# Attention and soft mixture of experts on one core: split diagonal blocks in the last batch, and a background piece that may wait for a change of matmul row form

## The chip, the cores and the metric

The kernel runs on one core of a Trainium2 chip. All times are device microseconds (us) of one execution; the clock of TensorE in the tables is the share of full speed that was granted. PE is TensorE, DVE is VectorE, ACT is ScalarE, SP is SyncE, whose queue issues every DMA of this kernel.

## The reference

```
u, v: (8, 2496, 256)   z: (8, 2496, 64)   phi: (256, 32)
w1: (8, 256, 1024)     w2: (8, 1024, 256)

attn = relu(z @ z.T / 2496) ** 2            # per batch, symmetric
x    = (u * (attn @ v)).reshape(19968, 256)

logits = x @ phi
d = softmax of logits over the tokens (columns), c = softmax over the 32 slots (rows)
slots = d.T @ x                             # 32 slots of 256, 4 for each of 8 experts
slots = per expert: relu(slots @ w1[e]) @ w2[e]
out   = c @ slots                           # (19968, 256) float32
```

## The kernel before, in words

**Chunks, blocks and half steps.** Each of the 8 batches has five chunks of queries (512, the last 448 wide) and five blocks of 512 keys. A block is worked off in two *half steps* of 256 keys, so a chunk has 10 half steps, a batch 50, the program 410 (the last batch's last chunk is cut in two). A half step consists of `prepare(k)`, which makes the squared scores of half k, and of the sums of `acc` over its keys. `prepare` runs three half steps ahead of the sums (two at the very start). Products are split in a high and a low part (`ph`, `pl`, and v and z alike), so each is three matmuls.

**Symmetry.** Scores of a block and chunk off the diagonal are made once; DVE transposes them (`y`), `store` writes them to DRAM (`turned_<chunk>_<block>`), and when the mirrored chunk needs them they are fetched (`r<-turned`). Such a half is `turned` and has no score matmuls. In the table `MEETS` a chunk's row gives the order of its key blocks. A block in the diagonal that is written as two pairs, as `(1, 0)` and `(1, 1)`, is in split form: its first half *lends* (DVE transposes the half that its mirror can use, `yd`, and `lend` stores it, `lent<-yd`), its second half *borrows* (`rd<-lent`) and makes scores over 256 queries instead of 512. `MEETS[0]` (batches 1 to 6, and most of batch 0) has all diagonals in split form, `MEETS[1]` (the last batch, whose blocks go in the order 4, 0, 1, 2, 3) none.

**Row forms of PE.** Where the half prepared in a step has scores of its own, the step's sums are `sums_halves`: pairs of matmuls over 64 rows, with the scores (64 rows too) between. Where it is turned, they are `sums_whole`: matmuls over 128 rows. In the timeline the tile column tells the form, 64\*128 or 128\*128.

**Background work.** As soon as 1024 tokens of x are complete, `groups(q)` puts 15 pieces in the list `work`: logits, the exponentials, four transposes of x and one of the weights, four shifts between other pieces, and a closing piece. One piece is taken in each half step but the first two of a chunk. A `shift` is four DMAs of 72 KB, `xt<-y`, on SP. The closing piece puts `slot_sums` in `late`; these products with `xt` are run by PE inside the *next* group's logits, after its own 32 matmuls, and need all four shifts of their group:

```
            if late:
                late.pop()(ps)
...
            todo = [logits, ex, *blocks, e, shifts[0], c0, shifts[1], c1, shifts[2], c2, shifts[3]]
            todo.append(lambda: (c3(), late.append(slot_sums)))
```

Logits and slot sums have a third form, 64\*32. From the last shift to the next group's logits are the closing piece and whatever time the list is empty. `logits` is always the first of its group.

**Order.** Every engine's instructions run in program order (`InOrder`), so a waiting instruction holds up all that follow on its engine. On SP stand, in a half step's order, what `transfers(h)` issues: u, fetches of turned and borrowed halves up to eight steps ahead, loads of the next batch's z and v (`splits`), stores; then the step's shift. `FIRST_Z` says after which half step the first batch's z blocks are split into high and low parts (two casts on ACT and two subtractions on DVE each).

Before the change all engine instructions stand under the helper's line L64, after it under L67.

Of the kernel before, what the change touches and what calls it, by code (L numbers as in the profile page):

```python
# [33 lines left out]
CATCH = 18  # L34
# [3 lines left out]
MEETS = (  # L38
# [3 lines left out]
)  # L42
FIRST_MEETS = ((0, 1, 2, 3, 4), (1, 0, 2, 4, 3)) + MEETS[0][2:]

FIRST_Z = {8: 1, 9: 2, 10: 4, 11: 3}

RAW_SCORES = 12

PAD = 224

# [17 lines left out]
def attn_soft_moe_kernel(ctx, tc, uT, v, zz, phi, ww, outT):  # L68
# [93 lines left out]
    def constants():  # L162
        make_identity(nc, ident)


        nc.gpsimd.memset(rsel, 0.0)
        for h in range(4):
            rows = slice(h * NS, (h + 1) * NS)
            nc.gpsimd.tensor_copy(ssel[rows], ident[rows, rows])
        for h in range(2):  # L170
            for r in range(4):
                nc.gpsimd.tensor_copy(
                    rsel[:, h, r, 16 * h : 16 * h + 16].rearrange("k (j s) -> k j s", s=SE),
                    ident.rearrange("k (j q) -> k j q", q=NS)[:, :, 0:SE],
                )
        sp.dma_start(phi_sb, phi.rearrange("(c p) s -> p c s", p=P))
        nc.gpsimd.memset(one, 1.0)
# [38 lines left out]
    halves = []  # L216
# [21 lines left out]
    def run(todo):  # L238
        now, todo[:] = todo[:], []
        for f in now:  # L240
            f()
# [17 lines left out]
    def scores(k):  # L259
# [21 lines left out]

        if k < RAW_SCORES:
            for h, rows in enumerate(HALF):
# [133 lines left out]
    def sums_halves(k, acc, phase, before):  # L417


        x = halves[k]  # L420
        todo = [[], []]
        hi, lo = pend[k]
        for t, kt in enumerate(x.tiles):
            vt = vt_[x.b, kt // 2][:, kt % 2]
            hh, lh, hl = (vt[:, 0], hi[:, t]), (vt[:, 1], hi[:, t]), (vt[:, 0], lo[:, t])
            if kt < KT - 1:
                for h in range(2):
                    todo[h] += [hh, lh, hl]
            else:

                todo[0] += [hh] if phase else [hh, lh]
                todo[1] += [hl] if phase else [lh, hl]
        for i in range(len(todo[0])):
            for h, rows in enumerate(HALF):
                vp, pp = todo[h][i]
                c = h ^ phase ^ side[0]
                mm = pe.matmul(
                    totals(acc, c, x), vp[rows, c * P : (c + 1) * P], columns(pp[rows], x),
                    start=(x.begins and phase == 0 and i == 0),
                    stop=(x.ends and phase == 1 and i == len(todo[0]) - 1),  # L440
                )
                if before is not None:
                    await_(mm, before)
                    before = None
        if phase == 0:
            turn = nc.gpsimd.nop()
            await_(turn, mm)
            return turn
        side[0] ^= 1

    def sums_whole(k, acc):

        x = halves[k]
        hi, lo = pend[k]
        for t, kt in enumerate(x.tiles):
            assert kt < KT - 1
            vt = vt_[x.b, kt // 2][:, kt % 2]
            for c in range(2):
                for i, (l, r) in enumerate(((0, hi), (1, hi), (0, lo))):
                    pe.matmul(  # L460
                        totals(acc, c, x), vt[:, l, c * P : (c + 1) * P], columns(r[:, t], x),
                        start=(x.begins and t == 0 and i == 0),
                        stop=(x.ends and t == 1 and i == 2),
                    )
# [41 lines left out]
    def groups(q):  # L506
# [103 lines left out]
        def turn_x_whole(i):  # L610
            j, t0 = i // 2, i % 2 * 2
            ps = ms_ps.tile([P, 2, 512], F32, tag="ms", name=f"xt_{q}_{i}")
            for k in range(2):
                turn_x(ps[:, k], x, 4 * j + t0 + k)
            for k in range(2):
                copy_x(act.copy, ps[:, k, 0:D], xt[:, t0 + k, j * D : (j + 1) * D])
# [38 lines left out]
        rest = lambda: None  # L655
        if q < NQG - 2:

            todo = [logits, ex, *blocks, e, shifts[0], c0, shifts[1], c1, shifts[2], c2, shifts[3]]
            todo.append(lambda: (c3(), late.append(slot_sums)))
        else:  # L660


            todo = [rest, rest, logits, ex, lambda: behind.append(adding.pop(0)), lambda: behind.append(add_counts)]
            todo += [c0, c1, c2, c3, turn_e_whole, *[lambda i=i: turn_x_whole(i) for i in range(4)]]
            todo.append(lambda: late.append(last_slot_sums))
# [69 lines left out]
    def weights(left):  # L735

        if left in W_TAKES:
            W_TAKES[left]()
        for i in W_LOADS.get(left, ()):
            load_w(i)  # L740
# [11 lines left out]
    work = []  # L752
# [14 lines left out]
    def transfers(h):  # L767

        x = halves[h]
        if x.at == 2:  # L770
            load_u(x.b, x.ch)
        for k in range(h + 1, min(h + 9, len(halves))):
            y = halves[k]

            if y.turned and y.opens and k not in arriving and k not in fetched:
                if k - h <= 7 and (y.b, y.p, y.ch[0]) in scratch:
                    fetched.add(k)
                    fetch(k)
            if y.borrows and k - h <= 5 and k not in fetched and (y.b, y.p, y.p) in scratch:
                fetched.add(k)  # L780
                borrow(k)
        for f, b, i in splits.get(h + 2, ()):
            if (b, 0) not in vt_:
                take_blocks(b)
            landing.setdefault(h + 2, []).append(f(b, i))
        while stores and stores[0][0] <= h + 1:
            stores.pop(0)[1]()

    def split_first_v():
        if v_splits:  # L790
            v_splits.pop(0)()
            open_loads(NRAW)
# [3 lines left out]
    def between_last(k):  # L796

        if k:
            if k == 1:
                xps.append(sc_ps.tile([P, 2, QC], F32, tag="sc", name="tr_first"))  # L800
                two = [raws.tile([P, 2, D], F32, tag="raw", name=f"xt_last_{i}", bufs=NRAW) for i in range(2)]
                xt_last.extend(t[:, i] for t in two for i in range(2))
            ps = xps[0][:, k - 1, 0:D]
            turn_x(ps, xg_[NQG - 1], k - 1)
            copy_x(act.copy, ps, xt_last[k - 1])
# [7 lines left out]
    def keep_busy(n):  # L813
        for _ in range(n):
            for h, rows in enumerate(HALF):
                pe.matmul(idle[:, h], zero[rows, 0:P], zero[rows], start=True, stop=True)
# [7 lines left out]
    prepare(1)  # L824
    keep_busy(5)
    constants()
    acc = None
    for h, x in enumerate(halves):
        if x.begins:
            acc = acc_ps.tile([P, 2, QC], F32, tag="acc", name=f"acc_{x.ch[3]}")  # L830
        last = len(halves) - h
        transfers(h)
        weights(last)
        for f in landing.pop(h, ()):
            behind.append(f)
        if work and (x.at > 1 or last <= 20):
            work.pop(0)()
        ahead = [k for k in range(h + 2 + (h > CATCH), h + 3 + (h >= CATCH)) if k < len(halves)]
        split_first_v()
        if ahead and not halves[ahead[0]].turned:  # L840
            turn = sums_halves(h, acc, 0, None)
            prepare(ahead.pop(0))
            sums_halves(h, acc, 1, turn)
        else:
            if ahead and not x.ends:
                prepare(ahead.pop(0))
            elif not ahead:
                run(middle)
                run(behind)
                between_last(3 - last)  # L850
            sums_whole(h, acc)
        if x.ends:
            finish_chunk(x.b, x.ch, acc)
        for k in ahead:
            prepare(k)
        if h in FIRST_Z:
            z_splits.pop(FIRST_Z[h])()
        del pend[h]
# [281 lines left out]
```

## Time and profile before

| | before |
|---|---|
| median of 3 runs | 1359.67 us (1359.03 to 1361.28) |
| the profiled execution | 1361.58 us |
| its span | 1359.8 us |
| mean granted clock of TensorE | 0.984 |
| busy: PE, DVE, ACT | 1336.1, 1084.2, 908.7 us |
| PE, sums of `acc` with the high and the low part | 988.4 and 622.7 us |
| PE, scores `sc` of two blocks and of one | 131.5 and 54.7 us |
| DMA: mean rate, written and read in HBM | 219 GB/s, 112.98 and 161.25 MB |
| `xt<-y`: DMAs, KB each, median from issue to landing | 288, 72.0, 3.4 us |
| `turned<-y`: the same | 320, 256.0, 4.4 us |
| `lent<-yd`: the same | 132, 64.0, 2.5 us |

In a row of the timeline stand the start, the duration, the engine, the line, the operation, what it writes and reads, the tile form, and how many instructions were drawn together; in brackets stands how long the engine was idle ahead of it and what ended that. Durations of matmuls overlap, so the pitch is read from the starts. A row of windows gives for each engine the busy time and the count, and at its end the granted clock, the busy share of the DMA engines and GB/s. PE is busy in 9 tenths or more of every one of 40 slices but the last two.

### The profile page before, as it was taken

What the parts mean: (1) busy time and instruction counts of PE and PEld (TensorE: products, weight loads), DVE (VectorE), ACT (ScalarE), POOL (GpSimd) and SP (SyncE); (2) the same over time, 40 slices, a digit from 0 to 9 for tenths busy, and PEclk for the clock granted to TensorE, in tenths of its full rate; (3) what the DMA queues carried; (4) which work ended last, traced back from release to release, by engine and by line L of the source; (5) the groups of instructions that cost most, each with busy time, mean ns of one, the idle gap of its engine ahead of it and who ended that gap; (6) DMA issues with size and microseconds to landing.
All of it is one profiled execution on the core that took longest, in us unless ns stands there. A gap on an engine that the chain in (4) does not pass through costs nothing.

```text
span 1359.8 us, 27351 instructions
## 1 busy us (share of the span) xinstructions
PE 1336.1 (98%) x10929; PEld 1062.3 (78%) x10929; DVE 1084.2 (80%) x1444; ACT 908.7 (67%) x1093; POOL 3.7 (0%) x22
## 2 busy tenths in 40 slices
PE   9999999999999999999999999999999999999985
PEld 6777887778777888778877788778877788778952
DVE  7878897779868898688987889797986889876563
ACT  8866686668755687566856678566875668654453
POOL 0000000000000000000000000000000000000000
PEclk9999999999999999999999999999999999999985
DMA  6568677675758667686776666777585776769969
GB/s 204 158 186 253 206 191 223 196 242 162 221 172 286 211 161 211 183 255 204 191 225 190 230 202 165 226 240 256 142 237 164 243 234 176 219 167 303 361 271 378
DMA packets 132511, 297.28 MB, mean 219 GB/s; under 512 B 17440, under 2 KB 36896, under 8 KB 120608
## 3 DMA queue, kind: packets, MB, share of 16 engines
q1 hardware_dynamic: 132384, 295.54, 70.6%
q8 instruction: 86, 1.41, 0.4%
q14 instruction: 41, 0.34, 0.1%
HBM read 161.25 MB, written 112.98 MB: 202 GB/s over the span
## 4 chain that ended last, share of the span: by engine, by line
PE 92%; ACT 2%; DMA 2%; DVE 2%; SPq 1%; issue 1%; DVEq 0%; ACTq 0%
PE acc L64 74%; PE sc L64 11%; PE lg L64 2%; PE pf L64 2%; SPq L64 1%; ACT r L64 1%; ACT ot L64 1%; PE po L64 1%; DMA lent<-yd 1%; PE h L64 1%; DMA outT<-ot 1%; DMA vr<-in_v 0%; ACT ph L64 0%; DVE pl L64 0%; PE idle L64 0%
## 5 line engine op out<-in xcount | busy, mean ns | idle before, releaser
L64 PE MATMUL acc<-ph,v 64*128 64x512 f32 (+5 forms) x5036 | 988.4, 387 | 0.0
L64 PEld LDWEIGHTS acc<-ph,v 64*128 64x128 f32 (+1 forms) x5036 | 593.5, 185 | 146.5 <-issue 24.9
L64 PE MATMUL acc<-pl,v 64*128 64x512 f32 (+5 forms) x2518 | 622.7, 383 | 1.5 <-DVE pl L64 1.5
L64 DVE TENSOR_TENSOR pl<-r,ph 128x1024 fp32r<-128x1024 f32 (+1 forms) x412 | 468.5, 1145 | 118.2 <-ACT ph L64 107.7
L64 ACT ACTIVATE r<-sc 128x1024 f32<-128x1024 f32 (+1 forms) x244 | 232.7, 954 | 194.6 <-PE sc L64 185.9
L64 ACT CAST ph<-r 128x1024 fp32r<-128x1024 f32 (+1 forms) x285 | 290.2, 1023 | 108.5 <-PE acc L64 77.1
L64 PEld LDWEIGHTS acc<-pl,v 64*128 64x128 f32 (+1 forms) x2518 | 306.8, 185 | 62.9 <-DVE pl L64 4.4
L64 ACT ACTIVATE r<-r 128x1024 f32<-128x1024 f32 (+1 forms) x244 | 241.1, 988 | 7.0
L64 DVE STREAM_TRANSPOSE y<-r 128x1024 f32<-128x1024 f32 x160 | 198.1, 1238 | 0.0
L64 PE MATMUL sc<-z,z 64*128 64x512 f32 x912 | 131.5, 393 | 0.2 <-ACT r L64 0.2
L64 DVE CAST ph<-r 128x1024 fp32r<-128x1024 f32 (+1 forms) x127 | 76.0, 598 | 40.9 <-ACT r L64 38.7
L64 PEld LDWEIGHTS sc<-z,z 64*128 64x128 f32 x912 | 85.0, 184 | 20.8 <-ACT r L64 0.6
L64 ACT CAST z<-zr 64x512 fp32r<-64x512 f32 x70 | 43.3, 619 | 56.2 <-DMA zr<-in_zz 55.0
L64 DVE TENSOR_TENSOR xg<-acc,ut 128x1024 f32<-128x1024 f32 (+7 forms) x57 | 48.4, 872 | 34.3 <-PE acc L64 34.3
L64 DVE TENSOR_TENSOR z<-zr,z 64x512 fp32r<-64x512 f32 x70 | 48.1, 687 | 21.5 <-ACT z L64 19.7
L64 DVE TENSOR_TENSOR v<-vr,v 128x512 fp32r<-128x512 f32 x80 | 53.6, 669 | 11.2 <-ACT v L64 11.1
L64 ACT CAST v<-vr 128x512 fp32r<-128x512 f32 x79 | 48.4, 613 | 17.9 <-DMA vr<-in_v 17.9
L64 PE MATMUL sc<-z 64*128 64x512 f32 (+1 forms) x468 | 54.7, 339 | 0.0
L64 DVE STREAM_TRANSPOSE y<-xg 128x512 f32<-128x512 f32 x72 | 49.5, 688 | 0.0
L64 PEld LDWEIGHTS sc<-z 64*128 64x128 f32 x468 | 41.1, 184 | 7.7
L64 DVE COPY ot<-pf 128x1024 f32<-128x1024 f32 (+2 forms) x22 | 24.3, 1103 | 21.9 <-PE pf L64 20.8
L64 ACT COPY ot<-pf 128x1024 f32<-128x1024 f32 (+2 forms) x22 | 20.1, 915 | 26.2 <-PE pf L64 24.7
(149 smaller groups left out, 481.0 us busy)
## 6 DMA issues: line engine op xcount, KB each, us to landing
turned<-y SPq DMA_DIRECT2D x320, 256.0 KB, 4.4
r<-turned SPq DMA_DIRECT2D x76, 1024.0 KB, 6.3
xt<-y SPq DMA_DIRECT2D x288, 72.0 KB, 3.4
vr<-in_v SPq DMA_DIRECT2D x80, 256.0 KB, 3.8
outT<-ot SPq DMA_DIRECT2D x16, 1024.0 KB, 6.9
ut<-in_uT SPq DMA_DIRECT2D x31, 512.0 KB, 5.3
zr<-in_zz SPq DMA_DIRECT2D x35, 256.0 KB, 5.5
lent<-yd SPq DMA_DIRECT2D x132, 64.0 KB, 2.5
```

Source lines behind the costliest of these rows:

```text
L64: return lambda *a, **k: self.tc.keep_in_program_order(f(*a, **k))
```

## The change

Three tables and one rule. In `MEETS[1]` three chunks of the last batch (their diagonal blocks 0, 1 and 2) get split diagonals, which also changes the order of their blocks. Two z splits of the first batch come one and two half steps later. And the logits of the groups 0 to 17 may now wait in the list, with all pieces behind them, for up to `HOLD` half steps, if within that time a half step comes whose row form differs from that of the step before (`switch`); they are run in that step.

```diff
-    ((0, 1, 2, 4, 3), (0, 4, 1, 2, 3), (0, 4, 1, 2, 3), (4, 2, 3, 0, 1), (0, 1, 2, 4, 3), (4, 3, 0, 1, 2)),
+    ((0, 1, 2, 4, 3), ((0, 0), 1, 4, 2, 3, (0, 1)), (0, (1, 0), 4, 2, 3, (1, 1)),
+     ((2, 0), 4, 3, (2, 1), 0, 1), (0, 1, 2, 4, 3), (4, 3, 0, 1, 2)),
...
-FIRST_Z = {8: 1, 9: 2, 10: 4, 11: 3}
+FIRST_Z = {8: 1, 9: 2, 11: 4, 13: 3}
...
+HOLD = 4
...
+            logits.meets_switch = True
             todo = [logits, ex, *blocks, e, shifts[0], c0, shifts[1], c1, shifts[2], c2, shifts[3]]
...
+    def ahead_of(h):
+        return [k for k in range(h + 2 + (h > CATCH), h + 3 + (h >= CATCH)) if k < len(halves)]
+
+    whole = [not k or halves[k[0]].turned for k in map(ahead_of, range(len(halves)))]
+    switch = [i and whole[i] != whole[i - 1] for i in range(len(halves))]
+    held = 0
...
         if work and (x.at > 1 or last <= 20):
-            work.pop(0)()
-        ahead = [k for k in range(h + 2 + (h > CATCH), h + 3 + (h >= CATCH)) if k < len(halves)]
+            if hasattr(work[0], "meets_switch") and True in switch[h : h + 1 + HOLD - held] and not switch[h]:
+                held += 1
+            else:
+                held = 0
+                work.pop(0)()
+        ahead = ahead_of(h)
```

The numbers behind the names are running numbers of tiles and differ between the programs. First PE, at the logits of group 4 in batch 2, chunk 1 (`lg_...<-xg` are its own products, `lg_...<-xt` the slot sums of group 3). Before:

```order
L64 MATMUL acc_4399<-ph_4335,v_4_3159 128x512 x4
L64 MATMUL acc_4399<-pl_4336,v_4_3159 128x512 x2
L64 MATMUL lg_4492<-xg_3567,phi_sb 32x256 x16
L64 MATMUL lg_4492<-xt 32x256 x16
L64 MATMUL acc_4399<-ph_4377,v_5_3160 128x512 x4
L64 MATMUL acc_4399<-pl_4378,v_5_3160 128x512 x2
```

After:

```order
L67 MATMUL acc_4390<-ph_4462,v_8_3163 128x512 x4
L67 MATMUL acc_4390<-pl_4463,v_8_3163 128x512 x2
L67 MATMUL lg_4622<-xg_3567,phi_sb 32x256 x16
L67 MATMUL lg_4622<-xt 32x256 x16
L67 MATMUL acc_4390<-ph_4506,v_6_3161 128x512 x2
L67 MATMUL acc_4390<-pl_4507,v_6_3161 128x512
```

The logits moved three half steps on, from between two steps of 64-row pairs (x4 and x2 on both sides) to the place where the pairs change to 128-row products (x2 and x1 behind).

Second SP, at the same place. Before, in batch 2:

```order
L64 DMA lent_1_4307<-yd_4297 32x4x128 x4
L64 DMA r_4441<-turned_0_1_3983 128x2048
L64 DMA turned_1_2_4443<-y_4339 32x4x512 x4
L64 DMA ut_4488<-in_uT 128x2x512
L64 DMA rd_4490<-lent_1_4307 128x512
L64 DMA r_4576<-turned_0_2_4076 128x2048
L64 DMA turned_1_4_4578<-y_4427 32x4x512 x4
L64 DMA r_4663<-turned_1_2_4443 128x2048
```

After, in batch 2:

```order
L67 DMA xt<-y_3878 32x576 x4
L67 DMA r_4432<-turned_0_1_3976 128x2048
L67 DMA turned_1_2_4434<-y_4327 32x4x512 x4
L67 DMA ut_4479<-in_uT 128x2x512
L67 DMA rd_4481<-lent_1_4294 128x512
L67 DMA r_4528<-turned_0_2_4067 128x2048
L67 DMA turned_1_4_4530<-y_4418 32x4x512 x4
L67 DMA xt<-y_3878 32x576 x4
L67 DMA r_4615<-turned_1_2_4434 128x2048
```

Before, in batch 3:

```order
L64 DMA xt<-y_6102 32x576 x4
L64 DMA r_6379<-turned_0_1_5890 128x2048
L64 DMA turned_1_2_6381<-y_6277 32x4x512 x4
L64 DMA ut_6426<-in_uT 128x2x512
L64 DMA rd_6428<-lent_1_6245 128x512
L64 DMA r_6474<-turned_0_2_6023 128x2048
L64 DMA turned_1_4_6476<-y_6365 32x4x512 x4
L64 DMA xt<-y_6102 32x576 x4
L64 DMA r_6561<-turned_1_2_6381 128x2048
```

The last two shifts of group 3 moved to this place in batch 2, where in the program before no shift stood; the order is now that of batch 3 before. The second shift shown is the one for which the slot sums in `lg_4622` wait.

## The prediction

> **What bounds the kernel now.** I read the busy times first: TensorE works for 98% of the span, so until the tail time is lost or won only where PE gets fewer columns, changes form less often, or stands still.
>
> ```profile
> PE 1336.1 (98%) x10929; PEld 1062.3 (78%) x10929; DVE 1084.2 (80%) x1444; ACT 908.7 (67%) x1093; POOL 3.7 (0%) x22
> L64 DVE STREAM_TRANSPOSE y<-r 128x1024 f32<-128x1024 f32 x160 | 198.1, 1238 | 0.0
> ```
>
> Then the timeline of PE. A change of row form has a price: two pairs at full pitch follow each other every 0.233 us (a 128-row product, or two 64-row ones). From 237.25 to 237.57 are 0.32 instead of 0.233, and 237.57 to 238.14 takes 0.57 for four 64-row products instead of 0.467, so this change from 128 to 64 rows costs 0.19. The logits and slot sums have a third form (64*32) and stand here inside a half step of 64-row sums.
>
> ```profile
> 237.25 0.39 PE L64 MATMUL acc<-pl,v 128*128 128x512 f32 x1
> 237.57 0.73 PE L64 MATMUL acc<-ph,v 64*128 64x512 f32 x4
> 238.14 0.39 PE L64 MATMUL acc<-pl,v 64*128 64x512 f32 x2
> ...
> 241.27 1.09 PE L64 MATMUL lg<-xg,phi_sb 64*32 64x256 f32 x32
> 242.16 1.07 PE L64 MATMUL lg<-xt 64*32 64x256 f32 x32
> ```
>
> The next rows give the way back (380.04 to 380.37 is 0.33, and 380.37 to 380.94 is 0.57: 0.20 together) and the price of score products over 512 and over 256 columns: six take 0.86 and 0.52.
>
> ```profile
> 375.46 0.86 PE L64 MATMUL sc<-z,z 64*128 64x512 f32 x6
> ...
> 378.50 0.52 PE L64 MATMUL sc<-z 64*128 64x256 f32 x6
> ...
> 380.04 0.40 PE L64 MATMUL acc<-pl,v 64*128 64x512 f32 x2
> 380.37 0.73 PE L64 MATMUL acc<-ph,v 128*128 128x512 f32 x2
> 380.94 0.39 PE L64 MATMUL acc<-pl,v 128*128 128x512 f32 x1
> ```
>
> Last, the waits. The only stall of PE near 1 us in mid-program is at 793, where a load of v went out at 783.83 because SP was busy with four shifts for 4.26 ahead of it; ACT waits 3.40 for its landing, DVE follows, and PE loses 1.07:
>
> ```profile
> 778.90 4.26 SPq L64 DMA_DIRECT2D xt<-y  x4
> ...
> 783.83 0.92 SPq L64 DMA_DIRECT2D vr<-in_v  x2
> ...
> 789.34 0.62 ACT L64 CAST v<-vr 128x512 fp32r<-128x512 f32 x1 [3.40 <-DMA vr<-in_v]
> 793.14 0.47 PE L64 MATMUL acc<-pl,v 64*128 64x448 f32 x2 [1.07 <-DVE pl L64]
> ```
>
> **The change part by part.** *Row form.* Counted in the order of the two programs, PE changes between whole and half steps, or to the logits and back inside one form, 115 times before and 106 after (11 logits come to stand at a change that is there anyway; the new order of the last batch has 2 changes more). 9 x 0.20 = -1.8 us; bounds -1.7 and -1.8 by the two prices.
>
> *Narrow diagonals.* Three second halves have six score products of 256 columns instead of 512: 3 x (0.86 - 0.52) = -1.0, all on PE's path. In return each lends and borrows: a half-wide transpose on DVE (half of 1.238), some smaller casts, four 64 KB stores and one fetch on SP. DVE's and ACT's cover is the slack of the last batch, 160.0 - 124.4 and 160.0 - 101.5:
>
> ```profile
> 1116.00:1276.00 160.00, 159.79 (x1395) 131.65 (x1392) 124.42 (x176) 101.45 (x126) 0.00 (x0) 1.00 0.76 227
> ```
>
> I cost it at nothing; without cover it would be three times about 0.6. The borrowed half comes five or more half steps after the lending one, so the stores have time.
>
> *Two z splits moved* (block 4 one half step later, block 3 two). A split is two subtractions on DVE, 1.40. Block 3's now falls between the casts of halves 15 and 16, where the remainder is ready at 63.84 + 1.23 = 65.07 and PE takes it at 66.03:
>
> ```profile
> 51.93 1.40 DVE L64 TENSOR_TENSOR z<-cw,z 64x512 fp32r<-64x512 f32 x2
> ...
> 63.84 1.23 DVE L64 TENSOR_TENSOR pl<-r,ph 128x1024 fp32r<-128x1024 f32 x1
> ```
> ```profile
> 66.03 0.40 PE L64 MATMUL acc<-pl,v 64*128 64x512 f32 x2
> ```
>
> 1.40 against 0.96 of slack: +0.4, bounds 0 (DVE has gaps just ahead) and +1.4.
>
> *The stall at 793.* The background pieces of the batches 2, 4 and 6 come later, so this shift no longer stands ahead of that load: -1.1, bounds -1.1 and 0 (another shift may meet another load).
>
> These four give -1.8 - 1.0 + 0.4 - 1.1 = -3.5.
>
> *The held logits.* A logits piece may wait up to four half steps for a change of form. Held with it are the other 14 pieces of its group and of the next one, since one list feeds one piece per half step. But inside the logits of group q PE also runs the slot sums of group q-1, which need the four DMAs of that group's last shift. Before, the last shift was issued at least five half steps ahead of them. Now the catching up runs the other way: when a group is late and the next logits then meet a change at once, only the closing piece of the old group stands between. By the order after, the distance is 9 for five groups, 4 or 5 for seven, and only **2 half steps** for the groups 4, 9, 14 (first type) and 5, 10, 15 (second type). All of PE is queued behind those slot sums, in program order: the sums of the half, its scores, and after them ACT, DVE and the next stores.
>
> The price of two half steps is in the trace: in the batches 3 and 5 of before, SP has at the same place of the batch (chunk 1) the very order that batches 2, 4 and 6 get now: shift, fetch, `turned_1_2`, fetch, `turned_1_4`, shift. PE comes to the change where the logits would stand at 538.27 in batch 3, and reaches slot sums 0.89 later (242.16 - 241.27): 539.16.
>
> ```profile
> 524.86 0.59 SPq L64 DMA_DIRECT2D xt<-y  x1
> 525.49 0.58 SPq L64 DMA_DIRECT2D r<-turned  x1
> 526.17 2.27 SPq L64 DMA_DIRECT2D turned<-y  x4
> ...
> 536.43 0.33 SPq L64 DMA_DIRECT2D r<-turned  x1
> 536.86 2.30 SPq L64 DMA_DIRECT2D turned<-y  x4
> 539.20 4.44 SPq L64 DMA_DIRECT2D xt<-y  x4
> ```
> ```profile
> 538.27 0.73 PE L64 MATMUL acc<-ph,v 128*128 128x512 f32 x2
> ```
> ```profile
> L64 SPq DMA_DIRECT2D xt<-y x4: 519/890/2004, 539.2 to 543.0; - x4
> DMA to landing us min/median/max: 3.3/5.6/6.5
> ```
>
> The last of the four shifts is issued at 543.0 and lands at 546.3 at the earliest (shortest landing 3.3): PE would stand 546.3 - 539.16 = 7.1. In batch 5 the same from 857.09 + 0.89 = 857.98 to 861.4 + 2.2 = 863.6: 5.6.
>
> ```profile
> 857.09 0.73 PE L64 MATMUL acc<-ph,v 128*128 128x512 f32 x2
> ```
> ```profile
> L64 SPq DMA_DIRECT2D xt<-y x4: 588/854/2022, 857.5 to 861.4; - x4
> DMA to landing us min/median/max: 2.2/3.0/5.3
> ```
>
> Mean 6.4, three times: **+19.1**. The lower bound is batch 2 itself in before, where `turned_1_4` was issued earlier:
>
> ```profile
> 373.94 4.03 SPq L64 DMA_DIRECT2D turned<-y  x4
> ```
>
> A shift behind it starts at 377.97, its last DMA 3.8 later (543.0 - 539.2), and lands 2.2 on, at 384.0; PE at 380.37 + 0.89 = 381.26: 2.7. I take 6.4, since there the row ahead of the store is a shift, as it will be, and here a store. For the second type the odd batches again have a shift at the place:
>
> ```profile
> 598.00 0.73 PE L64 MATMUL acc<-ph,v 64*128 64x512 f32 x4
> ```
> ```profile
> L64 SPq DMA_DIRECT2D xt<-y x4: 588/588/924, 595.2 to 597.5; - x4
> DMA to landing us min/median/max: 2.7/3.4/4.4
> ```
>
> 597.5 + 2.7 = 600.2 against 598.00 + 0.89 = 598.89: 1.3 each, **+3.9**; bounds 0 (the shift takes its turn a little sooner) and 597.5 + 4.4 - 598.89 = 3.0.
>
> The Trainium skill prices this landing too ("DMA: Bandwidth & Descriptors", the section on the fixed and variable cost): about 2.0 us plus the bytes at 436 GB/s, so by estimate 2.2 for 72 KB. By it the first stall would be 543.0 + 2.2 - 539.16 = 6.0 instead of 7.1 and the total about 1.7 lower; batch 3's own shortest landing is 3.3, so I keep the rows.
>
> *What a stall does afterwards.* The clock (third value from the end of a row of windows) shows it in the tail: a stretch in which PE worked 2.32 of 3.40 us is followed by one at 0.51, then full speed. The stall at 793, with 2.67 of 3.40 worked, left it at 1.00.
>
> ```profile
> 789.40:792.80 3.40, 2.67 (x15) 1.85 (x13) 2.75 (x5) 2.84 (x5) 0.00 (x0) 1.00 1.05 331
> ```
> ```profile
> 1303.10:1306.50 3.40, 2.32 (x41) 1.39 (x43) 1.87 (x4) 1.44 (x3) 0.00 (x0) 1.00 0.13 51
> 1306.50:1309.90 3.40, 3.40 (x30) 1.95 (x30) 1.25 (x2) 1.01 (x1) 0.00 (x0) 0.51 0.65 258
> 1309.90:1313.30 3.40, 3.40 (x62) 2.08 (x62) 2.31 (x2) 2.02 (x2) 0.00 (x0) 0.99 1.01 417
> ```
>
> So after each stall of the first type I expect 3.4 us at half clock, which lose 1.7: 3 x 1.7 = **+5.1**, bounds 0 and, if the shorter stalls of the second type do it too, 10.2. Stalls of 1.3 lie between the two rows and nearer the first, so I take none for them.
>
> **Sum.** -3.5 + 19.1 + 3.9 + 5.1 = +24.6 on the profiled execution, whose time is 1361.58 (span 1359.8). That is 1.91 above the median of the runs, so in their terms 1359.67 + 24.6 = **1384.3**.
>
> **Rivals.** *The clock does not fall.* All as above without the 5.1: 1379.2. For it: 1.07 us at 793 did nothing. Against: the row at 1306.50.
>
> *Short stalls.* The fetch ahead of `turned_1_4` is not held up, so the first type stands 2.7: 1384.3 - 3 x 3.7 = 1373.2, and 1368.1 if the clock stays. For it: batch 2 in before. Against: the batches with the order of after. The Trainium skill ("TensorE: Matmul & The Clock Gate", "HAM oscillation") would let the clock fall only for PE gaps over about 3.4 us. By that rule short stalls keep the clock and give this second time, 1368.1; the tail, where 1.08 of 3.40 was idle ahead of the half clock, speaks against it.
>
> *No stall: faster.* SP issues the last shift as soon as its data is there, so that its last DMA goes out by 539.16 - 2.2 = 537.0 in batch 3's time and no slot sums wait. Then only the -3.5 is left (1356.2), and from that point on every us later is paid three times. For it: SP waits in these places, so it has room. Against: six us are missing in both batches, with the same order.
>
> *The hold does nothing* can be excluded: the order of the changed program has the logits moved.
>
> **Chances.** Stalls with a fall of the clock as summed 0.50; without it 0.20; short stalls 0.19; no stall 0.07; a little of everything that cancels 0.04. The range reaches from short stalls whose clock falls at some of the three (1370) to all first-type stalls at 7.1 with a second half-clock stretch after the second type (about 1384.3 + 2.1 + 5.1 = 1391.5): 1370 to 1392. Anything within 0.2% (2.7 us, about what a measurement tells from no change) is called the same: faster 0.07, same 0.04, slower 0.89.
>
> **What would show it.** Right: in the groups of PE the row of slot sums (`lg<-xt`) has an idle time ahead of it of about 20 us in total, released by DMA xt, in three places at a change from half to whole in chunk 1 of the batches 2, 4 and 6 and smaller ones in chunk 3; the slices after them show a clock under 9 tenths; the changes of form are 9 fewer; the 1.07 at 793 is gone; the last batch's `sc<-z` has 256 columns three times more. Wrong: no idle time at `lg<-xt` (then the shifts are earlier than in batches 3 and 5), or PE stalls elsewhere, at a load of v or z that a moved shift now delays, or in the last batch at a borrowed half.

## The result: 3.8% slower

| | before | after |
|---|---|---|
| median of the runs | 1359.88 us (1359.03 to 1361.28, 4 runs) | 1411.86 us (1408.22 to 1413.13, 4 runs) |
| ratio, 95% interval | | 1.0377 (1.0364 to 1.0389) |
| the profiled execution, its span | 1361.58, 1359.8 us | 1408.22, 1406.4 us |
| mean granted clock of TensorE | 0.984 | 0.972 |

The forecast of 1384.3 (1370 to 1392) had the side and the kind of loss, and was 28 us short. The profiled execution of the changed kernel is the fastest of its four, so the traces show 46.6 of the some 52 us.

The two lines below are of the page after, the busy times and the group of slot sums; the third is the same group before, in the view by lines.

```profile
PE 1344.4 (96%) x10929; PEld 1069.1 (76%) x10929; DVE 1085.7 (77%) x1449; ACT 907.4 (65%) x1097; POOL 3.7 (0%) x22
...
L67 PE MATMUL lg<-xt 64*32 64x256 f32 x576 | 28.2, 460 | 37.8 <-DMA xt<-y 31.5
```
```profile
L64 PE MATMUL lg<-xt 64*32 64x256 f32 x576 | 19.6, 376 | 0.0
```

One group of PE went from no idle time at all to 37.8 us, and what ended it is the landing of shifts. The timeline of PE after has it in six places: the first, third and fifth row are the groups 4, 9 and 14, the others 5, 10 and 15.

```profile
384.79 2.96 PE L67 MATMUL lg<-xt 64*32 64x256 f32 x32 [5.58 <-DMA xt<-y]
...
452.95 2.56 PE L67 MATMUL lg<-xt 64*32 64x256 f32 x32 [6.23 <-DMA rd<-lent]
...
719.61 2.31 PE L67 MATMUL lg<-xt 64*32 64x256 f32 x32 [7.17 <-DMA xt<-y]
...
786.80 2.59 PE L67 MATMUL lg<-xt 64*32 64x256 f32 x32 [5.74 <-DMA xt<-y]
...
1053.48 2.41 PE L67 MATMUL lg<-xt 64*32 64x256 f32 x32 [6.80 <-DMA xt<-y]
...
1121.51 2.50 PE L67 MATMUL lg<-xt 64*32 64x256 f32 x32 [6.24 <-DMA xt<-y]
```

(The releaser `rd<-lent` in the second row is inferred by the profile; the products read `xt` alone.) The six places stood in the forecast, with 6.4 us for the first type and 1.3 for the second. Measured are 5.58 + 7.17 + 6.80 = 19.6 and 6.23 + 5.74 + 6.24 = 18.2. The rows hold a second loss: 32 slot sums take 2.3 to 3.0 us, where they take 1.07 before. Windows around the second place show why:

```profile
444.00:449.50 5.50, 2.72 (x40) 1.52 (x38) 1.69 (x3) 2.53 (x4) 0.00 (x0) 1.00 0.73 214
449.50:455.40 5.90, 2.45 (x32) 1.08 (x32) 3.77 (x5) 1.83 (x3) 0.00 (x0) 0.53 1.03 307
455.40:459.00 3.60, 3.60 (x33) 2.93 (x28) 1.65 (x6) 0.58 (x1) 0.00 (x0) 0.82 0.75 296
459.00:462.00 3.00, 3.00 (x30) 2.40 (x28) 0.36 (x1) 2.64 (x4) 0.00 (x0) 1.00 0.01 5
```

The clock (third value from the end) is at 0.53 already while PE still waits, stays low through the slot sums, and is back at 1.00 by 459.

And why the second type waits as long as the first: SP's queue there in the timeline, the logits of PE, and the view of the tile `xt`.

```profile
439.57 4.32 SPq L67 DMA_DIRECT2D xt<-y  x4
443.94 1.08 SPq L67 DMA_DIRECT2D zr<-in_zz  x2
445.11 0.38 SPq L67 DMA_DIRECT2D ut<-in_uT  x1
```
```profile
445.63 1.09 PE L67 MATMUL lg<-xg,phi_sb 64*32 64x256 f32 x32
```
```profile
L67 SPq DMA_DIRECT2D xt<-y x4: 512/590/593, 445.5 to 447.4; - x4
DMA to landing us min/median/max: 6.1/6.5/6.9
```

The last shift goes out from 445.5 on, as PE starts the logits, and behind two loads of z and one of u (256, 256 and 512 KB) it needs 6.1 to 6.9 us to land. The other two places of this type have the same order on SP. In the row of batch 3 that the forecast used it went out 2.8 us before PE came, and landed in 2.7 to 4.4. Both times the load of u went out just ahead; from issue to landing it took, after and before:

```profile
ut<-in_uT SPq DMA_DIRECT2D x1, 512.0 KB, 7.1
```
```profile
ut<-in_uT SPq DMA_DIRECT2D x1, 512.0 KB, 4.6
```

So u landed at 445.11 + 7.1 = 452.2 and the first DMA of the shift at 445.5 + 6.9 = 452.4, right behind it; before, at 599.4 (594.78 + 4.6) and 599.6 (595.2 + 4.4).

### The profile page after: what moved, and what is told of

It is laid out like the page before. It is cut to its first block, busy times and chain, and to the rows that moved or that the text cites. A ratio compares the mean times of both kernels' runs of the same rounds, so it can differ in the third digit from the quotient of the medians.

```text
span 1406.4 us, 27374 instructions
## 1 busy us (share of the span) xinstructions
PE 1344.4 (96%) x10929; PEld 1069.1 (76%) x10929; DVE 1085.7 (77%) x1449; ACT 907.4 (65%) x1097; POOL 3.7 (0%) x22
## 4 chain that ended last, share of the span: by engine, by line
PE 84%; DMA 9%; ACT 2%; DVE 2%; SPq 2%; issue 1%; ACTq 0%; DVEq 0%
PE acc L67 68%; PE sc L67 10%; DMA r<-turned 3%; PE lg L67 3%; DMA xt<-y 2%; SPq L67 2%; DMA turned<-y 1%; PE pf L67 1%; DMA outT<-ot 1%; ACT r L67 1%; PE po L67 1%; DVE y L67 1%; ACT ot L67 1%; PE h L67 1%; ACT ph L67 0%
## 5 line engine op out<-in xcount | busy, mean ns | idle before, releaser
L67 ACT CAST z<-zr 64x512 fp32r<-64x512 f32 x70 | 43.3, 619 | 60.6 <-DMA zr<-in_zz 59.3
L67 PE MATMUL lg<-xt 64*32 64x256 f32 x576 | 28.2, 460 | 37.8 <-DMA xt<-y 31.5
L67 ACT CAST v<-vr 128x512 fp32r<-128x512 f32 x79 | 48.5, 614 | 13.5 <-DMA vr<-in_v 13.5
L67 PEld LDWEIGHTS lg<-xt 64*32 64x32 f32 x576 | 14.0, 122 | 47.1 <-DMA xt<-y 35.0
```

Of the source, the lines that this page charges most:

```text
L67: return lambda *a, **k: self.tc.keep_in_program_order(f(*a, **k))
```

## The experiments

Each starts from the changed kernel. "Time" is the median, with the ratio to the kernel before on the same chip and its interval.

**1. The hold alone.**

```diff
-    ((0, 1, 2, 4, 3), ((0, 0), 1, 4, 2, 3, (0, 1)), (0, (1, 0), 4, 2, 3, (1, 1)),
-     ((2, 0), 4, 3, (2, 1), 0, 1), (0, 1, 2, 4, 3), (4, 3, 0, 1, 2)),
+    ((0, 1, 2, 4, 3), (0, 4, 1, 2, 3), (0, 4, 1, 2, 3), (4, 2, 3, 0, 1), (0, 1, 2, 4, 3), (4, 3, 0, 1, 2)),
...
-FIRST_Z = {8: 1, 9: 2, 11: 4, 13: 3}
+FIRST_Z = {8: 1, 9: 2, 10: 4, 11: 3}
```

> Old tables (MEETS and FIRST_Z of before), HOLD = 4. Theory: the whole loss is the six slot sums that stand two half steps behind their last shift; each leaves PE idle for some 6.3 us and then slow for some more, about 8.4 in all, and the hold saves 10 changes of row form (2.0) and the stall near 793 (1.1). So the time is that of the whole change or 1 us either way: 1408 to 1415. Rival: a part of what the forecast missed (27 us) sits in the last batch or in the moved z splits; then this kernel stays 10 us or more below the whole change, under 1402.

Time 1413.81, 1.0393 (1.0379 to 1.0408). As the theory says. The same group of slot sums on its page has

```profile
L66 PE MATMUL lg<-xt 64*32 64x256 f32 x576 | 27.9, 460 | 41.9 <-DMA xt<-y 34.2
```

HOLD = 4 stays in this kernel, and the loss stays with it. Together with the next experiment this puts the whole loss on the hold.

**2. The tables alone.**

```diff
-HOLD = 4
+HOLD = 0
```

> The new tables, HOLD = 0. Theory: narrow score products -1.0, two changes of form more in the last batch +0.4, z splits +0.4, one logits piece at a change anyway -0.2: 0.4 below the kernel before, 1358.5 to 1360.5, and no row of PE that waits for xt. Rival of the first run: 1365 or more, with PE idle in the last batch at a borrowed half.

Time 1359.16, 0.9996 (0.9988 to 1.0005): inside the expected 1358.5 to 1360.5, and not told apart from the kernel before. The three narrow diagonals do no harm at a borrowed half.

**3. Only the second type.**

```diff
-HOLD = 4
+HOLD = 3
```

> All of the change, HOLD = 3. By the order only the groups 5, 10, 15 (second type) are left at two half steps, the groups 4, 9, 14 stand at eight. Theory: each stall belongs to its own place, since SP reaches that shift late there whatever happened before: 3 x 8.3 = 25, less about 1.5 for the tables and the seven logits at a change: 1380 to 1387, with PE idle some 6.2 three times. Rival, the forecast's: the place itself costs 1.3 and is only made worse by the stall of the first type ahead of it: 1361 to 1366.

Time 1386.13, 1.0189 (1.0173 to 1.0205): the theory's 1380 to 1387, far from the forecast's price. PE waits for `xt` three times, 20.9 us in all and 7.2 at the longest (7.2 to 7.6 if counted from the start of the last product ahead). A place of the second type is slow by itself, without a stall ahead of it.

**4. The last shift one piece earlier.**

```diff
-            todo = [..., shifts[1], c1, shifts[2], c2, shifts[3]]
+            todo = [..., shifts[1], c1, shifts[2], shifts[3], c2]
```

> All of the change, but the last shift changes places with the piece ahead of it in the list, so the distance is three half steps instead of two. In chunk 1 this takes it out from behind the waiting fetch and the store turned_1_4. Theory (what counts is what stands ahead of the shift on SP): the first type vanishes, to 0 to 1 us of idle, because the shift then goes out some 8 us earlier; in the second type it only passes a load of z and of u, 1.6 us, so 4.6 us of idle are left: 3 x (4.6 + 2) = 20, 1373 to 1380 in all. Rival (the distance counts, in half steps): each of the six becomes shorter by one half step, 2.8 to 3.5 us, so 3 us of idle are left at all six places: 1380 to 1390.

Time 1369.15, 1.0068 (1.0054 to 1.0083): less than either expected. On its page PE waits

```profile
PE lg L67 <- DMA xt<-y: 6.2, 5, 2.1
```

6.2 us instead of 37.8, for one half step more of distance. So the distance in half steps is not the measure that the rival took it for (3 us left at each place); but the theory was wrong on the second type, too, where it left 4.6. The view of `xt` at the same place of batch 2 shows what it had not counted:

```profile
L67 SPq DMA_DIRECT2D xt<-y x4: 507/588/593, 438.0 to 439.8; - x4
DMA to landing us min/median/max: 2.0/2.6/3.1
```

The shift now goes out ahead of one load of z and the load of u. It goes out 1.6 us before PE starts the logits (439.54) instead of with it, and *lands in 2.0 to 3.1 instead of 6.1 to 6.9*. In the changed kernel it landed right behind the load of u; here u goes out behind it. That the load of u ahead is what made it slow fits both runs and the row of batch 3, but the load of z stands behind it here as well, so it is not shown which of the two counts. Why u itself took 7.1 us there and 4.6 in batch 3 is open, too: one more load of z went out ahead of it, and two fetches of 1 MB (448.67) instead of one behind it.

The windows around two of the places left show how long a wait the clock stands:

```profile
698.80:702.20 3.40, 2.15 (x64) 0.90 (x47) 3.26 (x8) 1.57 (x2) 0.00 (x0) 1.00 1.00 347
702.20:705.60 3.40, 3.40 (x23) 2.65 (x15) 3.16 (x9) 0.59 (x3) 0.00 (x0) 1.00 0.76 286
1079.00:1082.40 3.40, 1.34 (x35) 0.57 (x34) 0.18 (x1) 0.80 (x2) 0.00 (x0) 0.99 0.71 184
1082.40:1085.80 3.40, 3.40 (x36) 1.82 (x38) 3.12 (x6) 3.35 (x5) 0.00 (x0) 0.50 0.86 275
```

A wait of 1.25 us (first pair) leaves it at 1.00, one of 2.06 us (second pair) halves it for 3.4. Experiment 7 shows that the length alone does not decide.

**5. A hold of two half steps.**

```diff
-HOLD = 4
+HOLD = 2
```

> All of the change, HOLD = 2. By the order no slot sums stand nearer than four half steps behind their last shift, and four logits pieces (one without any hold) meet a change of form. Theory: four half steps are enough, since no place with four showed an idle PE in the changed kernel: the time without hold (1359.2) less 3 x 0.2: 1357.5 to 1359.5. Rival: four are not enough where SP is late: some 1 to 3 us of idle at several of the six places, 1361 to 1370.

Time 1357.99, 0.9986 (0.9977 to 0.9995): as the theory says, a little faster than before. No slot sums wait.

**6. All shifts first.**

```diff
-            todo = [..., e, shifts[0], c0, shifts[1], c1, shifts[2], c2, shifts[3]]
+            todo = [..., e, *shifts, c0, c1, c2]
```

> All of the change with HOLD = 4, but in the list the four shifts stand one after the other right after the transposes, ahead of c0, c1 and c2; so five half steps lie between the last shift and the slot sums where two did. Theory: no stall is left and the gains stay: 1359.2 without hold, less 10 changes of form (2.0) and the stall near 793 (0.5 to 1.1): 1355 to 1358. Rival: four shifts in successive half steps keep SP busy for up to 4 us each and hold up a fetch or a load behind them, so that ACT waits for it and PE for DVE: 1360 or more.

Time 1374.63, 1.0104 (1.009 to 1.0118): the rival. The slot sums wait for nothing any more, but PE's scores do, as its waits and the row of the slot sums show:

```profile
ACT v L67 <- DMA vr<-in_v: 28.0, 12, 5.2
...
PE sc L67 <- ACT r L67: 11.3, 8, 3.1
```
```profile
L67 PE MATMUL lg<-xt 64*32 64x256 f32 x576 | 19.3, 376 | 0.0
```

Shifts in successive half steps stand between the loads of v; ACT waits for them (28.0 us against 17.9 before and 13.5 in the changed kernel), empties the scores' bank late, and PE stands at the scores.

**7. PE busy through the stall.**

```diff
+            if q % 5 in (0, 4) and 3 < q < 16:
+                for _ in range(FILL):              # FILL = 6
+                    ...                # the logits' 16 products, into the slot sums' columns
             if late:
                 late.pop()(ps)
```

> All of the change; at the six places PE repeats the products of the logits six times (6 x 0.89 = 5.3 us, their result is overwritten by the slot sums), so it waits with work instead of idle. The shift lands when it did. Theory: the 2 us that each stall costs beyond its idle time are the half clock behind it; with PE kept busy the clock stays and 6 x 2 = 12 go: 1397 to 1403 against 1411.9. Rival: they are the wait for one shift DMA after another, or belong to DVE and ACT that start late: 1409 to 1414.

Time 1403.92, 1.0330 (1.0313 to 1.0347): 8 us less than the change, just beyond the expected 1397 to 1403. (The 16 products are 32 in the trace.) Two of the six waits were longer than the filler, which left PE idle for 1.67 and 2.53 us ahead of the slot sums, and the clock fell at these two places alone. Four places kept it, and 4 x 2 are the 8 us. At a third place PE stood for 1.89 us inside the filler, for nothing that the profile shows, and the clock stayed. First the rows of PE, then the windows behind the waits of 1.67 and of 1.89:

```profile
385.33 2.22 PE L68 MATMUL lg<-xt 64*32 64x256 f32 x32 [1.67 <-DMA xt<-y]
...
1050.21 2.81 PE L68 MATMUL lg<-xg,phi_sb 64*32 64x256 f32 x93 [1.89 <-issue]
1052.78 1.44 PE L68 MATMUL lg<-xt 64*32 64x256 f32 x32
```
```profile
386.43:389.80 3.37, 3.37 (x28) 2.08 (x14) 2.04 (x7) 0.35 (x1) 0.00 (x0) 0.50 0.96 250
...
1050.20:1053.60 3.40, 3.39 (x113) 2.54 (x119) 0.00 (x0) 0.00 (x0) 0.00 (x0) 1.00 0.41 104
```

The row at 1052.78 shows a smaller part of the loss: at full clock, too, the slot sums take 1.4 to 1.9 us at the four places instead of 1.07. That part is no matter of the clock; that they wait for one DMA of the shift after another fits it. Once more with a longer filler:

**8. The same with the hold of three and eight repeats, at the three places of the second type.**

```diff
-HOLD = 4
+HOLD = 3
-            if q % 5 in (0, 4) and 3 < q < 16:
+            if q in (5, 10, 15):
-                for _ in range(FILL):              # FILL = 6
+                for _ in range(FILL):              # FILL = 8
```

> As HOLD = 3 (1386.1, three stalls of 7.2 to 7.6 us), but at the three places PE repeats the products of the logits eight times, 8 x 0.89 = 7.1 us, so no gap of more than 1 us is left. Theory: what each stall costs beyond its idle time, 1.4 for slot sums that take 2.5 instead of 1.0 and 0.6 to 0.8 after them, is the half clock: 3 x 2.1 go, 1379 to 1381, and the slot sums take 1.0 to 1.3. Rival: it is the wait for one DMA after another: 1385 to 1388.

Time 1384.01, 1.0181 (1.0167 to 1.0195), in neither of the two expected ranges. It is 2 us less than in experiment 3, whose four runs alone reach from 1384.20 to 1390.05, so the two are not told apart. The places tell more than the sum. The second one, in experiment 3 and here:

```profile
768.50:772.60 4.10, 0.00 (x0) 0.01 (x1) 3.85 (x6) 2.42 (x4) 0.00 (x0) 0.55 1.02 276
772.60:775.10 2.50, 2.48 (x34) 1.08 (x34) 0.33 (x1) 0.00 (x0) 0.00 (x0) 0.50 1.01 422
```
```profile
770.00:774.60 4.60, 4.60 (x173) 3.12 (x157) 3.19 (x5) 1.26 (x3) 0.00 (x0) 1.00 1.06 336
774.60:776.00 1.40, 1.40 (x39) 0.80 (x34) 0.09 (x1) 0.00 (x0) 0.00 (x0) 1.00 0.96 398
```

Here the slot sums take 1.4 us at full clock (1.2 at the third place) instead of 2.5 at half. So the greater part of the time beyond the idle is the clock's; a wait for one DMA after another can explain no more than the 0.2 to 0.4 us above the usual 1.0. At the first place PE stopped inside the filler, with nothing to wait for in the profile:

```profile
446.47 3.31 PE L68 MATMUL lg<-xg,phi_sb 64*32 64x256 f32 x70 [2.23 <-issue]
```

The clock fell all the same, and this place took longer than with the stall. What stopped it is open.

**9. The shifts on GpSimd's queue.**

```diff
-    pe, act, dve, sp = (InOrder(tc, x) for x in (nc.tensor, nc.scalar, nc.vector, nc.sync))
+    pe, act, dve, sp, gp = (InOrder(tc, x) for x in (nc.tensor, nc.scalar, nc.vector, nc.sync, nc.gpsimd))
...
-            sp.dma_start(xt[32 * b : 32 * b + 32, a], src[32 * a : 32 * a + 32, b])
+            gp.dma_start(xt[32 * b : 32 * b + 32, a], src[32 * a : 32 * a + 32, b])
```

> All of the change, the shifts issued from GpSimd's queue instead of SP's. Their data (the transposes) is there several half steps before SP comes to them. Theory: with nothing ahead of them they land in time, no slot sums wait, and SP is relieved too: 1355 to 1358. Rival: issuing from there is slower or the transfers are late for the traffic and not for SP's order: PE still waits for xt at the six places, 1365 to 1410.

Time 1377.36, 1.0130 (1.0114 to 1.0145). Half of the theory holds: away from SP's order no slot sums wait (0.0 us of idle ahead of `lg<-xt`), at the same distance of two half steps. The rest is a wait that neither side had named. `sums_halves` hands the two halves of a bank over by an empty instruction on GpSimd (L449), for which PE's second phase waits, and this now stands behind shifts that wait for their data (the row of the sums of `acc` on the page, and GpSimd's waits):

```profile
L67 PE MATMUL acc<-ph,v 64*128 64x512 f32 (+5 forms) x5036 | 992.1, 388 | 14.4 <-POOLq L449 13.9
```
```profile
POOL xt L67 <- DVE y L67: 625.7, 11, 108.1
```

**10. A hold of two, z splits as before.**

```diff
-HOLD = 4
+HOLD = 2
-FIRST_Z = {8: 1, 9: 2, 11: 4, 13: 3}
+FIRST_Z = {8: 1, 9: 2, 10: 4, 11: 3}
```

> The new MEETS, HOLD = 2, and FIRST_Z as before. Theory: as HOLD = 2 with all of the change (1358.0), less the 0.5 that PE lost at half step 17 in every kernel with the moved z splits: 1357.0 to 1358.0, and no step of the half starts at 17. Rival: the step at 17 is made up later by slack, or has another cause: 1358.0 to 1358.6, or the step stays.

Time 1357.43, 0.9985 (0.9976 to 0.9994). In the range, and the step at half 17 is gone from the trace; but the ratio is that of experiment 5, so the 0.5 us could not be told in the time. These two are the only versions told apart from the kernel before as faster, by some 2 us.

**11. Three shifts in a row.**

```diff
-            todo = [..., e, shifts[0], c0, shifts[1], c1, shifts[2], c2, shifts[3]]
+            todo = [..., e, shifts[0], c0, *shifts[1:], c1, c2]
-FIRST_Z = {8: 1, 9: 2, 11: 4, 13: 3}
+FIRST_Z = {8: 1, 9: 2, 10: 4, 11: 3}
```

> The new MEETS, HOLD = 4, FIRST_Z as before; in the list c0 stays between the first and the second shift, and the second to the fourth shift stand one after the other ahead of c1 and c2, so four half steps lie between the last shift and the slot sums. Theory: with c0 kept in its place DVE and ACT are not pushed together as with all shifts first, and four half steps were enough with HOLD = 2: 1356 to 1358. Rival: three shifts in successive half steps still hold up the loads of z and v, ACT waits and PE with it: 1361 to 1373.

Time 1364.35, 1.0035 (1.0023 to 1.0047): the rival. Here the loads of z are late, as its waits show (ACT waited 55.0 us for them before and 59.3 in the changed kernel):

```profile
ACT z L67 <- DMA zr<-in_zz: 68.2, 17, 9.0
...
PE sc L67 <- ACT r L67: 4.4, 7, 0.7
```

## Why the prediction fell short

*Side and kind of loss: right.* The hold shrinks the distance from the last shift to the slot sums to two half steps at six places, PE stands there and its clock falls; experiments 1 and 2 put the whole loss on the hold.

*First type: right.* 19.1 us forecast, 19.6 measured: 5.58 to 7.17 a place, where the two rows gave 5.6 and 7.1. The batches 3 and 5, with the same order on SP, were the right rows. The rival of short stalls (2.7 each) is out.

*Second type: the step that failed.* 3.9 us were forecast, 18.2 measured. The neighbour that I took had a shift at the place, but not the same queue ahead of it. In batch 2 after, SP had issued two more shifts since the end of the chunk before (from 420.56 and 427.22), it came to the last one 2.7 us later against PE, and a second load of z stood directly ahead. Against the forecast's two figures: the last DMA of the shift went out at 447.4, 0.9 us after PE had come to the slot sums (445.63 + 0.89) and not 1.4 ahead, and landed in 6.1 us instead of 2.7. For the first type I had compared the orders row by row; here I compared the place alone. The bound of 3.0 each was taken from the longest landing of that same row, and so shared the error.

*The clock: right in kind, too small.* 5.1 were forecast, 1.7 at three places. The clock fell at all six, since all six waits were long, and each time for 6.8 us (381.61 to 388.43 at the first). The windows from the start of the slot sums to the end of the half clock, the first two of six and the sum of all:

```profile
384.79:388.43 3.64, 3.64 (x34) 1.55 (x35) 0.54 (x2) 0.00 (x0) 0.00 (x0) 0.50 0.89 221
452.95:456.70 3.75, 3.75 (x38) 2.12 (x40) 1.39 (x5) 0.00 (x0) 0.00 (x0) 0.50 1.00 413
...
sum 23.30, PE 23.30 PEld 12.78 DVE 8.51 ACT 0.00 POOL 0.00; mean PE 3.88 PEld 2.13 DVE 1.42 ACT 0.00 POOL 0.00
```

In 23.3 us at half clock PE does what takes 11.65 at full: 11.65 lost, 1.9 a place. That the clock falls at all was right in part by luck, for the row of the tail was no measure of a stall: there 1.08 us of idle went ahead of the half clock, but 1.25 in experiment 4 did nothing, and in the tail of experiment 3 the clock fell at 1318.46 after a stretch with 3.18 of 3.41 us worked. What lowers it in the tail is open.

*Together.* The two profiled executions differ by 46.6 where the sum had 24.6. Of these 22.0, 14.3 are the second type, some 6.5 the clock and 0.5 the first type.

*The small terms.* The trace has 9 changes of row form fewer, as forecast (84 instead of 93 among the sums of `acc`, the scores and the logits). Each logits piece at a change saves 0.19 from step to step in the trace, as forecast (0.20). The stall at 793 is gone, and the half step starts there move by 1.35 (1.1 forecast). The moved z split costs 0.5 at half step 17 (0.4), of which some 0.35 stay. In the last batch, from the start of its fourth half step to its last, the changed kernel gains 0.7 on the one before, against -1.0 + 0.4 forecast. In the time these terms add up to little: without hold the ratio is not told from 1, with a hold of two it is -0.14%.

## What to carry to other kernels

When a piece of work is held back, look at what the delay does to the distance between the *next* producer and its consumer: a list that feeds one piece a step has no slack to catch up, and the delay of one group comes off the lead of the following one. A price for such a distance, taken from another place, holds only where the queue ahead of the producer is the same row by row, transfers in flight included. And on a PE that is busy all the time, as here, a wait of some 2 us or more can be paid twice, once as idle and once more as clock.

## What the runs showed of the hardware

A shift of four DMAs of 72 KB landed in 2.0 to 3.1 us in one order of SP's queue and in 6.1 to 6.9 in another, where it landed right behind a load of u that itself took 7.1.

The clock of PE was halved after waits of 2.06 us (experiment 4) and 1.67 us (experiment 7), and not after 1.25 (experiment 4) and 1.89 us (experiment 7). So the length of the wait alone does not decide. The half clock lasted 3.4 us after the wait of 2.06 and 6.8 at the six places of the changed kernel, twice as long. "TensorE: Matmul & The Clock Gate" of the Trainium skill (section "HAM oscillation") gives as its abstract rule that PE should have no idle gaps over some 3.4 us; the runs here had the clock fall for less, so that for short waits the measurement decides.
